# Words in the making moved to PSUM, groups of 768 columns, one more buffer, and a plan with later transposes

## The chip, the core and the metric

The kernel runs on one core of a Trainium2 chip. The metric is the time of one execution on the device, in microseconds (us): the median of the runs.

## What is computed

An attention over clusters feeds two feed-forward layers. Everything is float32 but the four weight matrices, which come as 64-bit floats.

```python
# q, k, v: (2, 8, 768, 64); centroids: (8, 16, 64)
q_assign = np.argmax(np.einsum('bhsd,hcd->bhsc', q_n, c_n), axis=-1)   # *_n: rows divided by their norm
k_assign = np.argmax(np.einsum('bhsd,hcd->bhsc', k_n, c_n), axis=-1)
mask = q_assign[:, :, :, None] == k_assign[:, :, None, :]
scores = scale * np.matmul(q, k.transpose(0, 1, 3, 2))
scores = np.where(mask, scores, -1000000000.0)
attn = np.exp(scores - np.max(scores, axis=-1, keepdims=True))
attn = attn / (np.sum(attn, axis=-1, keepdims=True) + 1e-09)
x = ...  # np.matmul(attn, v), heads joined: (1536, 512)
h = x @ w_in;   x = (h * np.cos(h)) @ w_out                  # w_in (512, 2048), w_out (2048, 512)
h = x @ w2_in;  out = (h * (1 / (1 + np.exp(-h)))) @ w2_out
```

## The kernel before

Every float32 operand is split into a high and a low float16 half, and a product is three matmuls (high by high, high by low, low by high). The 1536 tokens are 12 tiles of 128, in seven units (`UNITS`): two of one tile and five of two tiles.

All work is written as tasks with an engine, a duration, what they depend on, a priority and the buffers they take. A planner (`Graph.run`) plays them through once, in the program that builds the kernel, and the order in which it starts them is the order of the instructions on each engine, fixed. The constants in `T` are shifts of priorities and, for tasks that two engines could do, handicaps: the engine that would end first by the planner's durations, plus the handicap, gets the task. The lowest priority number goes first. `HB`, `EB`, `GB`, `WB` and `LOB` handicap VectorE (against ScalarE in the first case, GpSimd in the others), `TB` handicaps VectorE against ScalarE, `KB`, `CB` and part of `XB` handicap ScalarE, the other part of `XB` GpSimd.

Attention, per tile and head (96 in all): scores on TensorE into a PSUM buffer `pb` (L890), the maximum on VectorE (L900), two tiny steps (L904, L905), the exponential on ScalarE into a buffer `e` (L919), its high half on ScalarE or VectorE (L926, L928), its low half on GpSimd or VectorE (L933, L935), a DMA transpose of both halves issued by SP (L512) into another buffer, and the product with the values (L943, 18 matmuls into `xn_ps`). The buffers for halves and transposed halves come from one pool of eleven, `gen`, 768 columns each, of which `LEAST` keeps some for each kind. L960, L967 and L969 scale the output of a tile and split it.

Layer one, per unit (`layer1_in`, `layer1_out`): groups of `EW` = 1024 columns of the hidden layer are filled in a PSUM buffer `pb` (L1019 to L1021, 12 matmuls for each 128 rows of the hidden layer), then go through L1034 (ScalarE), L1035 (VectorE), L1037 (ScalarE, the cosine), L1040 (VectorE), L1042 (ScalarE, high half) and L1043 (GpSimd or VectorE, low half); the PSUM buffer is held until L1040. The second product goes into `g2_ps` (L1077 to L1079). Layer two (`layer2`) does the like for 512 tokens at a time, with L1200 to L1206 between its products (L1190 to L1192 and L1221 to L1223); it begins when the attention's buffers are given back, the `SWAP` task.

Weights: each of the four matrices is loaded in 16 pieces of 512 columns by 128 rows as pairs of 32-bit words, and `conv` makes a float32 of each pair: pass one on VectorE (L692) shifts the high word into the destination, pass two (L694) puts the sign and exponent bit in, and then either a third pass on VectorE adds the upper bits of the low word (L701), or ScalarE makes a number of the low word (L698) and GpSimd adds it (L699). `LOW` says for how many pieces of every four of each matrix (order: w_in, w_out, second w_out, second w_in) it is the latter. The sums that give the scale of a weight matrix are taken by TensorE (L765) or by ScalarE (L436).

PSUM: three buffers `pb` of 1024 float32 columns for scores, PE transposes, sums and the first product of both layers; `g2_ps` and `xn_ps` of 512 columns.

Of the kernel before, what the change touches and what calls it, by code (L numbers as in the profile page):

```python
# [10 lines left out]
I32 = mybir.dt.int32  # L11
# [10 lines left out]
T = dict(PW_IN=-2428, PW_OUT=-477, PW_STEP=783, W_AHEAD=-382, KV0=-981, KSTEP0=-32964, V0=33297, Q0=262, KSTEP=-17295,  # L22
         PREP=-1180, PREPQ=1313, LD=4990, LOB=-0.03, WB=-2.09, HB=1.22, EB=0.63, KB=-13.72, GB=2.92, CB=2.75, XB=1.77,
         SB=0.5, L2B=0.5, PV=-1944, HI=1053, LO=13021, XP=-1707, G1=1614, GE=-20317, GC=-1920, G2=1781, GO=-4433,
         W2=5268, XD=-9186, TB=2, WH=50.28, GATE=0)
UNITS = [(0, 0, 1), (0, 1, 1), (0, 2, 2), (0, 4, 2), (1, 0, 2), (1, 2, 2), (1, 4, 2)]

LOW = (2,2,2,2)
# [13 lines left out]
EW = 1024  # L42
NE = 4
NGEN = 11

LEAST = {'stg':2,'natk':2,'ph':4,'pT':3}
# [60 lines left out]
class Task:  # L107
    __slots__ = ("opts", "deps", "pri", "acq", "use", "lat", "table", "n", "outs", "end", "start", "tag", "port")

    def __init__(self, opts, deps, pri, acq, use, lat, table, port):  # L110
        self.opts, self.pri, self.acq, self.lat, self.table, self.port = opts, pri, acq, lat, table, port
        self.use = list(dict.fromkeys([*acq, *use]))
        self.deps = [d for d in dict.fromkeys(deps) if d is not None]
        self.outs, self.end, self.start = [], None, None


class Graph:
# [21 lines left out]
    def run(self):  # L139
# [14 lines left out]
        while done < len(self.tasks):  # L154
# [21 lines left out]
            for t in ready:  # L176
# [46 lines left out]
                done_at = t.end + t.lat + self.HOP[e]  # L223
# [46 lines left out]
def fused_kernel(tc, q, k, v, cent, w1i, w1o, w2i, w2o, out, dbg=None):  # L270
# [4 lines left out]
    P = 128  # L275
# [24 lines left out]
    with tc.manual_schedule(), tc.tile_pool(name="dram", bufs=1, space=DRAM) as dpool:  # L300
# [382 lines left out]
        def conv(dst, acc, src, shape3, pri, dst_buf=None, pool=None, deps=(), dst_deps=(), add_low=False):  # L683
# [8 lines left out]
            a = add("DVE", dve(WC, True), lambda: DV.tensor_scalar(  # L692
                d(), word(1), 3, 0x3FFFFFFF, op0=ALU.logical_shift_left, op1=ALU.bitwise_and), [l, *dst_deps], pri, acq=ex, use=[w], port=True)
            b_ = add("DVE", dve(WC), lambda: DV.scalar_tensor_tensor(  # L694
                d(), word(1), -0x40000000, d(), op0=ALU.bitwise_and, op1=ALU.bitwise_or), [a], pri - 1, use=[w, *ex], port=True)
            if add_low:

                r_ = add("ACT", act(WC, SRC), lambda: AC.activation(out=word(0), in_=word(0).bitcast(U32), func=AF.Copy, scale=2.0 ** -29), [l], pri - 2, use=[w])  # L698
                c_ = add("POOL", pool2(WC) + 0.11, lambda: PO.tensor_tensor(d(), d(), word(0), op=ALU.add), [b_, r_], pri - 2, use=[w, *ex])  # L699
            else:  # L700
                c_ = add("DVE", dve(WC), lambda: DV.scalar_tensor_tensor(  # L701
                    d(), word(0), 29, d(), op0=ALU.logical_shift_right, op1=ALU.bitwise_or), [b_], pri - 2, use=[w, *ex], port=True)
# [79 lines left out]
        def w1_prep():  # L782
# [10 lines left out]
            for i in range(NW):  # L793
                r = raw[:, i * WC:(i + 1) * WC]
                pr = PW_IN + i * 25
                c_ = conv(lambda r=r: r, None, w_in_src(w1i, i), 0, pr, None, p_wg, add_low=i % 4 < LOW[0])
# [27 lines left out]
            for d in range(ND):  # L824
# [4 lines left out]
                for c in range(4):  # L829
                    r = lambda c=c, d=d: place[d](c)  # L830
                    c_ = conv(r, None, w_out_src(w1o, d, c), WC // P, pr + c, None, p_wx if c in WXC else None, dst_deps=dd[d], add_low=c < LOW[1])
# [21 lines left out]
        def w2_convert():  # L853

            for i in range(NW):
                fb = Buf(p_w2s)
                pr = 1e6 + i * 10
                t, tq = conv(lambda fb=fb: fb.ap, w2_mx[:, i:i + 1], w2o[i * P:(i + 1) * P, :].bitcast(I32), 0, pr, fb, dst_deps=x_free if 2 in WX else (), add_low=i % 4 < LOW[2])
# [10 lines left out]
        def attention(u):  # L869
# [5 lines left out]
            for ti in range(nq):  # L875
# [4 lines left out]
                for h in range(H):  # L880
# [51 lines left out]
                    else:  # L932
# [4 lines left out]
                                   2 * NT, [tl], pr, [hb], [], [pb_], NT * b + t < PET[2])  # L937

# [162 lines left out]
        def layer2(l1_last):  # L1101
# [9 lines left out]
            for i in range(NW):  # L1111
                r = slice(i * WC, (i + 1) * WC)
                ms += conv(lambda r=r: raw(r), mx0[:, i:i + 1], w_in_src(w2i, i), 0, base + i * 10 - T["W2"], None, p_ws2, [t_swap], add_low=i % 4 < LOW[3])
# [192 lines left out]
```

## Time and profile before

| | |
|---|---|
| median of 3 runs | 826.79 us (824.79 to 829.62) |
| profiled execution, whole time | 824.2 us |
| profiled execution, first to last instruction | 822.5 us |
| TensorE busy | 715.3 us (87%), 6744 matmuls |
| VectorE busy | 541.2 us (66%), 1094 instructions |
| ScalarE busy | 490.8 us (60%), 702 |
| GpSimd busy | 230.9 us (28%), 197 |

Busy times are of the profiled execution. The share of busy time over the whole span mixes stretches with different limits: the attention with layer one up to about 560 us, and layer two alone after that. PE is TensorE's matmuls, PEld its weight loads, DVE is VectorE, ACT is ScalarE, POOL is GpSimd, SP issues the DMAs.

### The profile page before, as it was taken

What the parts mean: (1) busy time and instruction counts of PE and PEld (TensorE: products, weight loads), DVE (VectorE), ACT (ScalarE), POOL (GpSimd) and SP (SyncE); (2) the same over time, 40 slices, a digit from 0 to 9 for tenths busy, and PEclk for the clock granted to TensorE, in tenths of its full rate; (3) what the DMA queues carried; (4) which work ended last, traced back from release to release, by engine and by line L of the source; (5) the groups of instructions that cost most, each with busy time, mean ns of one, the idle gap of its engine ahead of it and who ended that gap; (6) DMA issues with size and microseconds to landing.
All of it is one profiled execution on the core that took longest, in us unless ns stands there. A gap on an engine that the chain in (4) does not pass through costs nothing.

```text
span 822.5 us, 16553 instructions
## 1 busy us (share of the span) xinstructions
PE 715.3 (87%) x6744; PEld 487.2 (59%) x6744; DVE 541.2 (66%) x1094; ACT 490.8 (60%) x702; POOL 230.9 (28%) x197
## 2 busy tenths in 40 slices
PE   2486677988779887899999999995999999999998
PEld 1353346777668765787787788882444444444443
DVE  7889988888789788989779756668670044004400
ACT  3769787888867766779659655548770045004400
POOL 3321634265452355346337323330000000000000
PEclk9967898999998999999999999997999999999999
DMA  8925799899999979978977986442312000000000
GB/s 273 358 71 160 196 196 189 148 167 187 177 183 195 248 146 174 176 194 176 183 163 127 214 183 216 141 132 75 104 51 77 26 1 0 26 26 1 0 26 26
DMA packets 233900, 111.27 MB, mean 135 GB/s; under 512 B 199520, under 2 KB 221536, under 8 KB 233824
## 3 DMA queue, kind: packets, MB, share of 16 engines
q1 hardware_dynamic: 233824, 110.23, 60.7%
q8 instruction: 52, 0.85, 0.4%
q14 instruction: 24, 0.20, 0.1%
HBM read 50.36 MB, written 10.49 MB: 74 GB/s over the span
## 4 chain that ended last, share of the span: by engine, by line
PE 58%; DVE 14%; DMA 13%; ACT 5%; issue 5%; POOL 2%; SPq 2%; POOLq 0%; DVEq 0%; ACTq 0%
DMA gen<-gen 7%; PE pb L1191 5%; PE pb L1192 5%; PE pb L1190 5%; PE pb L1019 4%; PE pb L1021 4%; PE pb L1020 4%; PE xn_ps L943 3%; PE pb L890 3%; DVE small L900 3%; PE xn_ps L1221 3%; PE g_ps L1221 3%; PE xn_ps L1223 3%; PE xn_ps L1222 3%; PE g_ps L1222 3%
## 5 line engine op out<-in xcount | busy, mean ns | idle before, releaser
L933 POOL TENSOR_TENSOR gen<-e,gen 128x768 f16<-128x768 f32 x67 | 110.0, 1656 | 63.4 <-ACT gen L926 47.3
L1078 PE MATMUL g_ps<-gT,w 128*128 128x256 f16 (+1 forms) x448 | 111.1, 260 | 3.3 <-POOL gT L1043 3.3
L919 ACT ACTIVATE e<-pb,small 128x768 f32<-128x768 f32 x96 | 94.7, 990 | 31.3 <-DVE small L905 11.9
L1019 PE MATMUL pb<-xT,w 128*128 128x256 f16 (+1 forms) x448 | 111.3, 260 | 1.8 <-DMA xT<-e 1.6
L1077 PE MATMUL g_ps<-gT,w 128*128 128x256 f16 (+1 forms) x448 | 111.2, 260 | 0.9 <-ACT x2s L1084 0.9
L1020 PE MATMUL pb<-xT,w 128*128 128x256 f16 (+1 forms) x448 | 111.2, 260 | 0.0
L1021 PE MATMUL pb<-xT,w 128*128 128x256 f16 (+1 forms) x448 | 111.2, 260 | 0.0
L1079 PE MATMUL g_ps<-gT,w 128*128 128x256 f16 (+1 forms) x448 | 111.2, 260 | 0.0
L900 DVE TENSOR_REDUCE small<-pb 128x1 f32<-128x768 f32 x96 | 89.3, 950 | 19.0 <-PE pb L890 17.0
L1202 DVE SCALAR_TENSOR_TENSOR e<-e,pb 128x1024 f32<-128x1024 f32 x24 | 29.3, 1219 | 105.2 <-ACT e L1200 105.1
L890 PE MATMUL pb<-kst,qst 96*128 96x512 f16 (+3 forms) x384 | 80.2, 343 | 18.0 <-ACT e L919 9.7
L943 PE MATMUL xn_ps<-vst,gen 128*128 128x64 f16 x1728 | 68.5, 196 | 21.5 <-DMA gen<-gen 19.8
L943 PEld LDWEIGHTS <-gen 128*128 128x128 f16 x1728 | 63.1, 100 | 33.5 <-DMA gen<-gen 26.4
L1190 PE MATMUL pb<-x2T,w 128*128 128x512 f16 x192 | 73.7, 384 | 4.5 <-ACT x2T L1170 4.5
L1043 POOL TENSOR_TENSOR gT<-e,gT 128x1024 f16<-128x1024 f32 x24 | 52.2, 2176 | 89.3 <-ACT gT L1042 80.4
L1191 PE MATMUL pb<-x2T,w 128*128 128x512 f16 x192 | 73.7, 384 | 2.5 <-DVE x2T L1172 2.5
L1192 PE MATMUL pb<-x2T,w 128*128 128x512 f16 x192 | 73.6, 383 | 0.0
L926 ACT ACTIVATE gen<-e 128x768 f16<-128x768 f32 x87 | 70.4, 840 | 2.1 <-DMA gen<-gen 0.9
L890 PEld LDWEIGHTS <-qst 128*128 128x128 f16 (+1 forms) x384 | 37.1, 101 | 41.7 <-issue 23.1
L1077 PEld LDWEIGHTS <-w 128*128 128x128 f16 x448 | 44.2, 99 | 9.8 <-issue 2.2
L1079 PEld LDWEIGHTS <-w 128*128 128x128 f16 x448 | 44.2, 99 | 7.8 <-issue 3.9
L1019 PEld LDWEIGHTS <-w 128*128 128x128 f16 x448 | 44.5, 99 | 5.6 <-DMA xT<-e 1.8
(201 smaller groups left out, 1515.0 us busy)
## 6 DMA issues: line engine op xcount, KB each, us to landing
ws<-in_moe_w_out_dram SPq DMA_DIRECT2D x24, 512.0 KB, 4.3
gT<-in_moe_w_in_dram SPq DMA_DIRECT2D x16, 512.0 KB, 5.7
ws<-in_moe_w_in_dram SPq DMA_DIRECT2D x16, 512.0 KB, 3.9
xT<-in_moe_w_out_dram SPq DMA_DIRECT2D x8, 512.0 KB, 4.8
w_dram<-x2s SPq DMA_DIRECT2D x16, 256.0 KB, 3.0
st<-w_dram SPq DMA_DIRECT2D x8, 512.0 KB, 4.4
gen<-in_k_dram SPq DMA_DIRECT2D x8, 384.0 KB, 6.7
gen<-in_v_dram SPq DMA_DIRECT2D x8, 384.0 KB, 5.2
```

What stands on the lines that cost most here:

```text
L890: PE.matmul(out=sbk.ap[:, c0:c1], lhsT=qs.ap[:kk, a, h], rhs=kb.ap[:kk, a, j].rearrange("p t c -> p (t c)")[:, c0:c1], start=(a == 1), sto ...
L900: DV.tensor_reduce(out=sm.ap[:, 0:1], in_=sbk.ap[:, :S], axis=AX.X, op=ALU.max, negate=True)
L943: PE.matmul(out=o, lhsT=hb.ap[:, pi, kt], rhs=vb.ap[:, vi, j, kt], start=(kt == 0 and pi == 0 and vi == 0), stop=(kt == NT - 1 and pi == 1 ...
L1019: PE.matmul(out=o, lhsT=wh[:, d, fs], rhs=xb.ap[:, 0, d, :n], start=(d == 0), stop=False)
L1020: PE.matmul(out=o, lhsT=wh[:, d, fs], rhs=xb.ap[:, 1, d, :n], start=False, stop=False)
L1021: PE.matmul(out=o, lhsT=wl[:, d, fs], rhs=xb.ap[:, 0, d, :n], start=False, stop=(d == ND - 1))
L1077: PE.matmul(out=o, lhsT=wh, rhs=gh, start=(f == 0 and i == 0), stop=False, skip_group_check=True)
L1078: PE.matmul(out=o, lhsT=wh, rhs=gl, start=False, stop=False, skip_group_check=True)
L1079: PE.matmul(out=o, lhsT=wl, rhs=gh, start=False, stop=(f == NF - 1), skip_group_check=True)
L1190: PE.matmul(out=o, lhsT=wh[:, d, fs], rhs=x[:, 0, d], start=(d == 0), stop=False)
L1191: PE.matmul(out=o, lhsT=wh[:, d, fs], rhs=x[:, 1, d], start=False, stop=False)
L1192: PE.matmul(out=o, lhsT=wl[:, d, fs], rhs=x[:, 0, d], start=False, stop=(d == ND - 1))
```

## The change

- `conv` gets a parameter `via`. With it, pass one writes into a PSUM buffer `pb` (512 of its columns), pass two reads and writes it there, and the last VectorE pass writes the destination. `VIA = (4,4,0,4)`, in the order of `LOW`, says for how many pieces of every four: all of w_in, w_out and the second w_in, none of the second w_out.
- `LOW` goes from (2,2,2,2) to (2,1,1,1).
- `EW` goes from 1024 to 768: the groups of layer one become three tiles of 256 columns (or six of 128), those of layer two 512 columns. The four `e` buffers get as much smaller; `gen` gets a twelfth buffer, and four instead of three are kept for transposed halves.
- In the planner a task has a field `more`: the transposes of the probabilities end 0.8 us later for what depends on them (`LATE`). It changes the plan's order alone.
- All of `T`'s constants are others.

```diff
-T = dict(PW_IN=-2428, PW_OUT=-477, PW_STEP=783, W_AHEAD=-382, KV0=-981, KSTEP0=-32964, V0=33297, Q0=262, KSTEP=-17295,
-         PREP=-1180, PREPQ=1313, LD=4990, LOB=-0.03, WB=-2.09, HB=1.22, EB=0.63, KB=-13.72, GB=2.92, CB=2.75, XB=1.77,
-         SB=0.5, L2B=0.5, PV=-1944, HI=1053, LO=13021, XP=-1707, G1=1614, GE=-20317, GC=-1920, G2=1781, GO=-4433,
-         W2=5268, XD=-9186, TB=2, WH=50.28, GATE=0)
+T = dict(PW_IN=-24521, PW_OUT=-778, PW_STEP=537, W_AHEAD=-7221, KV0=502, KSTEP0=-11826, V0=2122, Q0=-2053,
+         KSTEP=-4635, PREP=-1178, PREPQ=1321, LD=-18274, LOB=-0.79, WB=1, HB=1, EB=5, KB=-3.59, GB=1.71, CB=0.8,
+         XB=-1.49, SB=0.71, L2B=46.67, PV=-2908, HI=4830, LO=8647, XP=5755, G1=1860, GE=-4285, GC=-1560, G2=2315,
+         GO=-1529, W2=18407, XD=17052, TB=11.35, WH=-0.64, GATE=0)
+
+LATE = 0.8
...
-LOW = (2,2,2,2)
+LOW = (2,1,1,1)
+
+VIA = (4,4,0,4)
...
-EW = 1024
+EW = 768
 NE = 4
-NGEN = 11
-
-LEAST = {'stg':2,'natk':2,'ph':4,'pT':3}
+NGEN = 12
+
+LEAST = {'stg':2,'natk':2,'ph':4,'pT':4}
...
-                done_at = t.end + t.lat + self.HOP[e]
+
+                done_at = t.end + t.lat + self.HOP[e] + t.more
...
-            a = add("DVE", dve(WC, True), lambda: DV.tensor_scalar(
-                d(), word(1), 3, 0x3FFFFFFF, op0=ALU.logical_shift_left, op1=ALU.bitwise_and), [l, *dst_deps], pri, acq=ex, use=[w], port=True)
-            b_ = add("DVE", dve(WC), lambda: DV.scalar_tensor_tensor(
-                d(), word(1), -0x40000000, d(), op0=ALU.bitwise_and, op1=ALU.bitwise_or), [a], pri - 1, use=[w, *ex], port=True)
+            if via:
+
+                mb = Buf(p_pb)
+                m = lambda: mb.ap[:, :WC].bitcast(I32)
+                a = add("DVE", dve(WC), lambda: DV.tensor_scalar(
+                    m(), word(1), 3, 0x3FFFFFFF, op0=ALU.logical_shift_left, op1=ALU.bitwise_and), [l], pri, acq=[mb], use=[w])
+                to, td, tu = (d, dst_deps, ex) if add_low else (m, (), [])
+                b_ = add("DVE", dve(WC), lambda: DV.scalar_tensor_tensor(
+                    to(), word(1), -0x40000000, m(), op0=ALU.bitwise_and, op1=ALU.bitwise_or), [a, *td], pri - 1, acq=tu, use=[w, mb])
+            else:
...
             if add_low:
...
+            elif via:
+                c_ = add("DVE", dve(WC), lambda: DV.scalar_tensor_tensor(
+                    d(), word(0), 29, m(), op0=ALU.logical_shift_right, op1=ALU.bitwise_or), [b_, *dst_deps], pri - 2, acq=ex, use=[w, mb])
...
+                    if NT * b + t >= PET[2]:
+                        tt.more = LATE
```

## Rows read from the trace of the kernel before

**Rows 1.** Page of the kernel before: its span

```profile
span 822.5 us, 16553 instructions
```

**Rows 2.** Stage table of the whole span, all engines

```profile
core 0: us, PE busy (x) PEld busy (x) DVE busy (x) ACT busy (x) POOL busy (x), PEclk, DMA share, GB/s
0.00:150.00 150.00, 96.11 (x990) 64.19 (x991) 130.27 (x327) 106.99 (x156) 51.34 (x73) 0.86 0.78 206
150.00:350.00 200.00, 167.85 (x2376) 138.41 (x2374) 171.14 (x394) 151.74 (x236) 92.80 (x71) 0.96 1.01 179
350.00:500.00 150.00, 143.64 (x1721) 121.42 (x1719) 115.56 (x217) 109.67 (x168) 67.43 (x43) 1.00 0.89 183
500.00:575.00 75.00, 64.03 (x538) 52.88 (x537) 51.48 (x91) 45.22 (x70) 19.34 (x12) 0.93 0.40 127
575.00:822.50 247.50, 243.65 (x1129) 110.29 (x1127) 72.77 (x67) 77.22 (x76) 0.00 (x0) 1.00 0.09 30
```

**Rows 3.** TensorE's waits, 0 to 600 us: us in total, times, longest

```profile
PE xn_ps L943 <- DMA gen<-gen: 19.8, 20, 2.6
PE g_ps L765 <- POOL w L699: 12.2, 4, 7.7
PE pb L1190 <- ACT x2T L1170: 4.5, 1, 4.5
```

**Rows 4.** DMA transposes (line L512): us from issue to landing

```profile
DMA to landing us min/median/max: 3.1/4.4/7.0
```

**Rows 5.** Single lines of code: ns min/median/max, first and last start

```profile
L692 DVE TENSOR_SCALAR w<-ws x18: 408/424/2214, 93.2 to 556.6; 128x512 int32<-128x512 int32 x18
L694 DVE SCALAR_TENSOR_TENSOR x2s<-ws,x2s x16: 680/692/697, 141.5 to 485.3; 128x512 int32<-128x512 int32 x16
L960 DVE TENSOR_TENSOR e<-xn_ps,small x12: 679/688/692, 122.7 to 482.2; 128x512 f32<-128x512 f32 x12
L1035 DVE SCALAR_TENSOR_TENSOR e<-e,cols,pb x24: 1270/1279/1292, 149.0 to 535.9; 128x1024 f32<-128x1024 int32 x24
```

**Rows 6.** Stage table of L692, then L694 alone: VectorE busy us (instructions)

```profile
0.00:150.00 150.00, 17.76 (x33) 0.86 0.78 206
0.00:150.00 150.00, 26.49 (x33) 0.86 0.78 206
```

**Rows 7.** Timeline of GpSimd and VectorE around two moments: start us, us

```profile
41.18 1.35 POOL L699 TENSOR_TENSOR w<-w,gT 128x512 int32<-128x512 int32 x1 [3.27 <-DVE w L694]
41.42 1.66 DVE L694 SCALAR_TENSOR_TENSOR w<-gT,w 128x512 int32<-128x512 int32 x1
517.98 2.13 POOL L1043 TENSOR_TENSOR gT<-e,gT 128x1024 f16<-128x1024 f32 x1 [1.84 <-ACT gT L1042]
518.18 2.21 DVE L692 TENSOR_SCALAR w<-ws 128x512 int32<-128x512 int32 x1 [3.45 <-DMA ws<-in_moe_w_in_dram]
```

**Rows 8.** Groups by line, whole span: busy us, mean ns | idle before

```profile
L699 POOL TENSOR_TENSOR w<-w,ws 128x512 int32<-128x512 int32 x9 | 11.9, 1324 | 32.1 <-DVE w L694 30.0 <-DMA xf<-x_dram 1.5 <-issue 0.7
L698 ACT ACTIVATE ws<-ws 128x512 int32<-128x512 uint32 x20 | 13.5, 674 | 3.7 <-DMA ws<-in_moe_w_out_dram 2.1 <-DMA ws<-in_moe_w_in_dram 1.6
L1034 ACT ACTIVATE e<-pb,cols 128x1024 int32<-128x1024 f32 x24 | 26.6, 1108 | 27.8 <-PE pb L1021 25.3 <-DVE gen L935 2.4
L1040 DVE SCALAR_TENSOR_TENSOR e<-e,pb 128x1024 f32<-128x1024 f32 x24 | 29.2, 1217 | 7.7 <-ACT e L1037 7.7
L1227 ACT ACTIVATE x2s<-g_ps,cols 128x512 f32<-128x512 f32 x6 | 4.1, 687 | 48.8 <-PE g_ps L1223 48.8
L933 POOL TENSOR_TENSOR gen<-e,gen 128x768 f16<-128x768 f32 x67 | 110.0, 1656 | 63.4 <-ACT gen L926 47.3 <-DVE gen L928 8.9 <-PE pb L890 6.7
L935 DVE TENSOR_TENSOR gen<-e,gen 128x768 f16<-128x768 f32 x29 | 29.0, 1021 | 1.3 <-ACT gen L926 1.3
L969 DVE TENSOR_TENSOR e<-e 128x512 f16<-128x512 f32 x11 | 8.9, 808 | 0.0
```

**Rows 9.** TensorE's waits, 350 to 575 us alone

```profile
PE xn_ps L943 <- DMA gen<-gen: 6.3, 8, 1.2
```

## What the change should do to the time

> **What bounds the kernel now.** The span of the profiled execution is 822.5 us [rows 1]. I read the stage table first, which cuts it into five stretches [rows 2]. From 575 us to the end TensorE is busy for 243.65 of 247.5 us at full granted clock: the second layer, its queue full, VectorE and ScalarE below a third. From 350 to 500 us TensorE is busy 143.64 of 150. From 0 to 350 us it is different: VectorE is busy 130.27 of 150 and 171.14 of 200, together 301.4 of 350 (86%), TensorE less than that, and in the first 150 us its clock is granted at 0.86. So VectorE, with the chains that go through it, sets the first 350 us, TensorE everything after, with a seam at 500 to 575.
>
> The list of waits comes second [rows 3]. What TensorE loses, apart from sheer lack of work early on, is 19.8 us in 20 waits of the probability product (L943) for a transposed tile to land, 12.2 us in 4 waits of the weight sums (L765) for a GpSimd addition, and, at the seam, 4.5 us before the first matmul of layer two. There are 96 such transposes; they land 3.1 to 7.0 us after issue, median 4.4 [rows 4]: the spread is what a written-out order can't know.
>
> Third come the rows of single lines, for prices [rows 5 to 8], and the waits of the last stages alone [rows 9].
>
> **Part 1: words in PSUM (VIA).** In three of the four weight conversions, 48 of 64 pieces, the word in the making lies in a PSUM buffer between passes. Pass one (L692) has a median of 0.424 us from SBUF to SBUF [rows 5]. No row shows it into PSUM: it may stay at 0.42, or cost what a 512-column pass over PSUM costs, 0.688 us at L960 [rows 5]. I take the dear end, being the row with the same memory: +0.26 each. In the first 150 us lie 33 pieces [rows 6], 32 of them to move (all of layer one's): 32 x 0.26 = +8.4 us of VectorE.
> What comes back is lock time. At 41.18 us GpSimd begins an addition, at 41.42 a second pass (L694) that takes 1.66 instead of 0.69 us; at 517.98 another, and a first pass beside it takes 2.21 us [rows 7]. The 33 first passes before 150 us sum to 17.76 us, 3.8 above 33 x 0.424; the 33 second passes to 26.49, 3.7 above 33 x 0.69 [rows 5, 6]. L1035, one input in SBUF and one in PSUM, ran 24 times between 1270 and 1292 ns [rows 5]: never held up. So up to 7.5 us comes back, at least none; I take 7. Net +1.4 us before 150 us, bounds -7.5 to +8.4.
> The Trainium skill, "VectorE: DVE Perf Modes", section "Why PSUM operands drop a tier", speaks against this part: an fp32 operand in PSUM loses the two-fold speed. Its table of cycles for PSUM to SBUF gives, as an estimate, (120 + 512) / 0.96 = 658 ns; by that the passes cost 32 x 0.23 = +7.5 us instead of 8.4, with the same sign. No row here has shown that operation yet.
>
> **Part 2: fewer words summed on GpSimd (LOW 2,2,2,2 to 2,1,1,1).** Twelve pieces change: each loses 0.674 us on ScalarE (L698) and 1.324 us on GpSimd (L699) [rows 8] and gains a third pass of 0.69 us on VectorE. Four lie in w1_out (+2.8 us of VectorE in the first 150), four in the idle-time conversion of w2_out (+2.8 between 150 and 490), four at the seam (part 6). It shortens what the weight sums wait for: of their 12.2 us [rows 3], those before w1_in's end stay (LOW[0] is unchanged); I take 2 us of 12.2, on the path only if VectorE is not late too, so 0.
>
> **Part 3: EW 1024 to 768.** Layer one goes from 24 groups to 36: a unit of 256 tokens has six groups instead of four (the sixth of one tile), one of 128 has three instead of two. Columns stay. What is added is the fixed cost per instruction. ScalarE: 1.108 us at 1024 columns, 0.687 at 512, so 0.27 fixed [rows 8]; three of them times 12 are 9.7 us. VectorE: L1040 takes 1.217 at 1024, L960 0.688 at 512, so 0.16 fixed [rows 5, 8]; two of them times 12 are 3.8 us, half before 350. GpSimd adds little. Layer two doubles from 24 groups to 48 with 512 columns each: 48 x 0.27 + 48 x 0.16 = 20 us on engines that have 170 us to spare there [rows 2]. TensorE covers it: a group needs 12 matmuls, 2.5 us at the rate of layer two's 3 x 384 in 243.65 us. Nothing on the path; if the cover went, it would show as waits of L1190 for PSUM.
>
> **Part 4: the choices of engine (T).** The planner picks for many steps the engine that ends first plus a handicap. EB goes from 0.63 to 5: the low halves that VectorE takes (29 of 1.021 us, L935) go mostly to GpSimd, 1.656 us each (L933) [rows 8]. XB goes from 1.77 to -1.49: the 11 low halves of the attention output (0.808 us, L969 [rows 8]) leave VectorE too. HB and GB lean a little towards VectorE. I take 20 us and 9 us off, 13 back on: -16, bounds -35 to +5. GpSimd rises from 230.91 us by 20 x 1.66, less part 2's 16: it has room, being at 46% in its busiest stretch [rows 2].
> VectorE to 500 us then: +1.4 + 5.6 + 3.8 - 16 = -5 us, bounds -40 to +20. Before 350 VectorE is 86% of time, so **about -4 us** of time.
>
> **Part 5: later landing (LATE 0.8), one more general buffer (NGEN 12), four for transposed tiles.** Every planned product moves 0.8 us further behind its transpose, and SP's queue order follows. The 20 waits average 0.99 us: what 0.8 can remove lies between nothing (other waits take their place) and 16 us. In 350 to 575 us lie 6.3 us of them [rows 9] where TensorE is the bound: I take 5. Of the 13.5 before, where VectorE is late as well, I take 5. **-10 us.** A product put off holds its transposed buffer longer; the fourth one and the twelfth buffer are cover for that. Without them scores would stall behind L926.
>
> **Part 6: the seam.** The 16 conversions of layer two's first weights run beside the last unit of layer one; 16 x 0.26 + 4 x 0.69 = +7 us of VectorE, which is busy 51.48 of 75 us [rows 2], so most is covered. Fewer GpSimd steps shorten four of the chains. I take **+1 us**, bounds -6 (the 4.5 us wait and some of the slow clock, 0.93 in that stretch, gone) to +7.
>
> **Sum.** -4 - 10 + 1 = -13 us on the profiled execution's 824.2: 811.2. The median of the runs shown, 826.8, lies 2.6 above that execution, so the forecast for it is 814.
>
> **The rivals.**
> *Slower: PSUM buffers run short.* Scores, transposes, sums and layer one share three buffers of 1024 columns. Each word in the making now takes one for two or three passes, 1.4 to 2.1 us plus whatever VectorE does between. That is 48 x 2 = 96 us of one buffer, two thirds of it in the first 150 us. If TensorE then stands without a buffer in half the cases, and nothing hides it, 24 x 2 = 48; as VectorE, the bound there, would be at work on the same piece, half of that counts: +24, less the 13: about 837. It decides from the point where two other buffers are held when a word takes the third: layer one's groups hold one for fill plus four evacuations, some 8 us, so the seam is exposed too. Against it: TensorE has long gaps early that aren't for lack of PSUM. 0.24.
> *No change: waits move.* VectorE gets free, but the order is still fixed, and landing late was not the cause but the last of several things; the 19.8 us come back as waits for L919 or L926, GpSimd's 1.656 us in place of 1.021 in the chain of each tile eats the rest. 824 to 830, say 826. This is also the case in which LATE doesn't do what it says, a plan that would have the same products in the same places. 0.16.
> *More than forecast.* VectorE at -25 us with the full 16 us of landing waits: 824.2 - 22 - 16 + 2.6 = 789; half-way to my forecast, 799. 0.13.
>
> **How the numbers follow.** Forecast 0.47, with 804 to 822 as its own range. Faster by over 0.5% (below 822.7, about what a measurement of this kernel can tell): 0.47 + 0.13 = 0.60; same 0.16; slower 0.24. The range reaches half-way into the better case and half-way into the slow one and leaves out some 0.07 below and 0.12 above: 799 to 837.
>
> **What the profile after should show.** L692 and L694 writing `pb`, 0.66 to 0.69 us each, with no row above 1 us (part 1 right); at 0.42 my price was too dear. L699 at 20 instead of 32. L935 far below 29, VectorE below 300 us in the first 350. Waits of L943 for transposes under 8 us in total (part 5 right); if they are still near 20, or L890 waits as much longer, part 5 is wrong. Layer two within 1 us of 247. Wrong would be the whole if TensorE waits for conversions or PSUM buffers in the first 190 us (slow rival).

## The result and the profile after

| | before | after |
|---|---|---|
| median of 6 runs each, same chip | 827.35 us (824.79 to 829.62) | 818.98 us (818.15 to 822.83) |
| profiled execution, whole time | 824.2 us | 819.1 us |
| first to last instruction | 822.5 us | 817.4 us |

The ratio is 0.9904 (0.9878 to 0.993): about 8 us, 1.0%, faster. The forecast was 814, its range 799 to 837.

The page of after, then its stage table (columns as in [rows 2]):

```profile
span 817.4 us, 16847 instructions
...
PE 708.8 (87%) x6744; PEld 484.3 (59%) x6744; DVE 538.4 (66%) x1138; ACT 489.0 (60%) x762; POOL 298.4 (37%) x249
```

```profile
core 0: us, PE busy (x) PEld busy (x) DVE busy (x) ACT busy (x) POOL busy (x), PEclk, DMA share, GB/s
0.00:150.00 150.00, 92.97 (x903) 59.98 (x904) 127.54 (x341) 101.09 (x145) 63.59 (x89) 0.94 0.76 204
150.00:350.00 200.00, 170.91 (x2561) 145.34 (x2559) 165.57 (x381) 156.96 (x254) 116.79 (x83) 0.97 1.06 191
350.00:500.00 150.00, 145.46 (x1696) 123.14 (x1695) 109.88 (x213) 111.07 (x184) 86.42 (x58) 1.00 0.87 179
500.00:575.00 75.00, 60.95 (x488) 47.95 (x487) 59.24 (x104) 42.90 (x69) 22.43 (x14) 0.91 0.36 114
575.00:817.40 242.40, 238.55 (x1106) 107.94 (x1103) 76.13 (x101) 76.94 (x112) 9.13 (x6) 1.00 0.09 30
```

Against [rows 2]: VectorE's first 350 us fall from 301.4 to 293.1, GpSimd rises everywhere before 500 us (whole span 230.9 to 298.4), and the clock granted in the first 150 us rises from 0.86 to 0.94.

The stages are cut at fixed times and hide where the time went. Three events cut the span by work instead. They are the eighth and the twelfth (last) transpose of a tile's attention output that SP issues, and the first matmul of layer two. The rows of before, from the timelines of SP and TensorE (start us, us):

```profile
357.53 1.24 SPq L971 DMA_TRANSPOSE xT<-e  x1
...
485.46 1.24 SPq L971 DMA_TRANSPOSE xT<-e  x1
...
564.87 0.59 PE L1190 MATMUL pb<-x2T,w 128*128 128x512 f16 x1 [4.53 <-ACT x2T L1170]
```

The same in after:

```profile
349.45 1.23 SPq L992 DMA_TRANSPOSE xT<-e  x1
...
477.49 1.23 SPq L992 DMA_TRANSPOSE xT<-e  x1
...
555.88 0.59 PE L1211 MATMUL pb<-x2T,w 128*128 128x512 f16 x1 [3.74 <-ACT x2T L1191]
```

By the eighth tile after is 8.1 us ahead. The next 128.0 us are as long as before (127.9), the seam from the last transpose to layer two's first matmul goes from 79.4 to 78.4, and layer two, from that matmul to the end, from 257.6 to 261.5. So -8.0, -1.0 and +3.9 make the -5.1 of the two profiled spans.

The 8 us are not gained in the first 150 us, where most of the words are made. At the second tile's transpose after is 7.9 us behind (before first, then after), at the sixth it is level, 283.74 us against 283.32:

```profile
149.10 1.24 SPq L971 DMA_TRANSPOSE xT<-e  x1
157.04 1.48 SPq L992 DMA_TRANSPOSE xT<-e  x1
```

From the sixth to the eighth tile both kernels start the same 64 matmuls for scores and 288 into `xn_ps`, and 772 (before) and 759 (after) matmuls in all. Before needs 74.2 us for that, after 65.7 (columns as in [rows 2]), and no piece that `VIA` moves is converted there:

```profile
283.32:357.53 74.21, 62.03 (x779) 50.88 (x776) 65.26 (x154) 48.92 (x75) 31.89 (x23) 0.95 0.95 185
283.74:349.45 65.71, 60.32 (x759) 50.82 (x760) 56.58 (x142) 51.62 (x85) 37.98 (x27) 0.97 1.05 191
```

VectorE is busy 8.7 us less there. Three low halves of probabilities (L935, 2.7 us) and two of the attention output (L969, 1.4 us) have gone to GpSimd, and twelve one-column steps take a third of their time (before, then after):

```profile
L1061 DVE SCALAR_TENSOR_TENSOR cols<-cols 128x1 f32<-128x1 f32 x12 | 4.8, 471 | 0.0
L1082 DVE SCALAR_TENSOR_TENSOR cols<-cols 128x1 f32<-128x1 f32 x12 | 1.0, 154 | 0.0
```

Kernels below that share an order agree: 73.8 us in the kernel before with groups of 512 in layer two, 65.9 and 66.3 us in the two kernels on the seam. So this gain belongs to the order and the choices of engine; which of them makes it is not shown.

TensorE's waits from 0 to 600 us in after (us in total, times, longest), those that answer to [rows 3], with L1212, the second matmul group of layer two, and L908, which waits for a PSUM buffer:

```profile
PE xn_ps L964 <- DMA gen<-gen: 21.5, 21, 3.2
PE g_ps L783 <- POOL w L714: 16.0, 7, 7.9
PE pb L908 <- ACT e L937: 8.4, 7, 2.4
PE pb L1212 <- DVE x2T L1193: 6.5, 1, 6.5
...
PE pb L1211 <- ACT x2T L1191: 3.7, 1, 3.7
```

Waits for transposed tiles to land are 21.5 us, not fewer than the 19.8 of before.

The conversions in after (ns min/median/max, first and last start), to set beside [rows 5]: L701 and L704 are the first and second pass with the word in PSUM, L716 the third, L707 and L709 the first two with the word still in SBUF (the second w_out).

```profile
L701 DVE TENSOR_SCALAR pb<-ws x24: 675/689/697, 24.7 to 546.5; 128x512 int32<-128x512 int32 x24
L701 DVE TENSOR_SCALAR pb<-gT x16: 685/695/696, 5.0 to 44.8; 128x512 int32<-128x512 int32 x16
L701 DVE TENSOR_SCALAR pb<-xT x8: 675/690/714, 49.8 to 131.0; 128x512 int32<-128x512 int32 x8
L704 DVE SCALAR_TENSOR_TENSOR pb<-ws,pb x16: 678/695/697, 55.1 to 547.3; 128x512 int32<-128x512 int32 x16
L716 DVE SCALAR_TENSOR_TENSOR w<-ws,pb x13: 678/686/687, 103.3 to 548.0; 128x512 int32<-128x512 int32 x13
L707 DVE TENSOR_SCALAR x2s<-ws x16: 416/420/1616, 133.1 to 467.2; 128x512 int32<-128x512 int32 x16
L709 DVE SCALAR_TENSOR_TENSOR x2s<-ws,x2s x16: 673/684/1994, 148.4 to 467.7; 128x512 int32<-128x512 int32 x16
```

A first pass into PSUM costs 0.69 us, and none of the 48 took longer than 0.714; those that still write SBUF cost 0.42, and the longest took 1.616. And the low halves of the probabilities, against 67 and 29 in [rows 8] (busy us, mean ns): all 96 are GpSimd's.

```profile
L951 POOL TENSOR_TENSOR gen<-e,gen 128x768 f16<-128x768 f32 x96 | 159.2, 1672 | 70.4 <-ACT gen L944 27.3 <-DVE gen L946 18.5 <-issue 5.8
```

### The profile page after: what moved, and what is told of

Same layout as the page of the kernel before. It is cut to its first block, busy times and chain, and to the rows that moved or that the text cites. A ratio compares the mean times of both kernels' runs of the same rounds, so it can differ in the third digit from the quotient of the medians.

```text
span 817.4 us, 16847 instructions
## 1 busy us (share of the span) xinstructions
PE 708.8 (87%) x6744; PEld 484.3 (59%) x6744; DVE 538.4 (66%) x1138; ACT 489.0 (60%) x762; POOL 298.4 (37%) x249
## 4 chain that ended last, share of the span: by engine, by line
PE 57%; DVE 17%; DMA 13%; ACT 5%; issue 4%; POOL 2%; SPq 1%; ACTq 0%; DVEq 0%; POOLq 0%
DMA gen<-gen 8%; PE pb L1212 5%; PE pb L1213 5%; PE pb L1211 5%; PE xn_ps L964 3%; PE pb L908 3%; PE g_ps L1098 3%; PE g_ps L1099 3%; PE g_ps L1100 3%; DMA qst<-natq 3%; PE pb L1040 3%; PE pb L1042 3%; PE pb L1041 3%; PE xn_ps L1244 3%; PE xn_ps L1243 3%
## 5 line engine op out<-in xcount | busy, mean ns | idle before, releaser
L951 POOL TENSOR_TENSOR gen<-e,gen 128x768 f16<-128x768 f32 x96 | 159.2, 1672 | 70.4 <-ACT gen L944 27.3
L937 ACT ACTIVATE e<-pb,small 128x768 f32<-128x768 f32 x96 | 94.5, 988 | 25.2 <-DVE small L922 15.8
L1040 PE MATMUL pb<-xT,w 128*128 128x256 f16 (+1 forms) x448 | 108.9, 257 | 0.5 <-DVE e L1061 0.3
L1042 PE MATMUL pb<-xT,w 128*128 128x256 f16 (+1 forms) x448 | 108.9, 257 | 0.0
L1041 PE MATMUL pb<-xT,w 128*128 128x256 f16 (+1 forms) x448 | 108.9, 257 | 0.0
L1223 DVE SCALAR_TENSOR_TENSOR e<-e,pb 128x512 f32<-128x512 f32 x48 | 32.7, 684 | 94.0 <-ACT e L1221 94.0
L908 PE MATMUL pb<-kst,qst 96*128 96x512 f16 (+3 forms) x384 | 79.3, 337 | 14.7 <-ACT e L937 8.4
L964 PE MATMUL xn_ps<-vst,gen 128*128 128x64 f16 x1728 | 67.2, 196 | 21.6 <-DMA gen<-gen 21.5
L1064 POOL TENSOR_TENSOR gT<-e,gT 128x768 f16<-128x768 f32 (+2 forms) x36 | 54.5, 1523 | 67.9 <-ACT gT L1063 66.1
L1212 PE MATMUL pb<-x2T,w 128*128 128x512 f16 x192 | 73.6, 384 | 6.5 <-DVE x2T L1193 6.5
L944 ACT ACTIVATE gen<-e 128x768 f16<-128x768 f32 x81 | 66.2, 838 | 0.5 <-DMA gen<-gen 0.3
L908 PEld LDWEIGHTS <-qst 128*128 128x128 f16 (+1 forms) x384 | 36.5, 100 | 37.9 <-issue 20.7
L1227 DVE SCALAR_TENSOR_TENSOR w<-e,w 128x512 f16<-128x512 f32 x48 | 34.7, 726 | 24.6 <-ACT w L1225 24.3
L1225 ACT ACTIVATE w<-e 128x512 f16<-128x512 f32 x48 | 30.1, 628 | 31.5 <-DVE e L1223 31.4
L1098 PEld LDWEIGHTS <-w 128*128 128x128 f16 x448 | 43.9, 98 | 8.4
```

Of the source, the lines that this page charges most:

```text
L908: PE.matmul(out=sbk.ap[:, c0:c1], lhsT=qs.ap[:kk, a, h], rhs=kb.ap[:kk, a, j].rearrange("p t c -> p (t c)")[:, c0:c1], start=(a == 1), sto ...
L951: tl = add("POOL", pool2(S), lambda hi=hi, lo=lo, ex=ex: PO.tensor_tensor(lo(), ex(), hi(), op=ALU.subtract), [th], pr + T["LO"], use=[*eu ...
L964: PE.matmul(out=o, lhsT=hb.ap[:, pi, kt], rhs=vb.ap[:, vi, j, kt], start=(kt == 0 and pi == 0 and vi == 0), stop=(kt == NT - 1 and pi == 1 ...
L1040: PE.matmul(out=o, lhsT=wh[:, d, fs], rhs=xb.ap[:, 0, d, :n], start=(d == 0), stop=False)
L1041: PE.matmul(out=o, lhsT=wh[:, d, fs], rhs=xb.ap[:, 1, d, :n], start=False, stop=False)
L1042: PE.matmul(out=o, lhsT=wl[:, d, fs], rhs=xb.ap[:, 0, d, :n], start=False, stop=(d == ND - 1))
```

## The experiments

Ratios are to the kernel before on the same chip, with 95% intervals; after itself has 0.9904. In the first three kernels every other instruction keeps its place in the order of after (or of before), so that only the part named differs. In the two on the seam that holds for TensorE up to the seam, where VectorE's order changes too. In the others the planner makes a new order. Stretches are from one profiled execution each; in kernels with the same order the attention's end differs by up to 1.6 us.

### The words back in SBUF, the order kept

```diff
+        mids = [[x2s[:, :WC].bitcast(I32), x2s[:, WC:].bitcast(I32)], []]
...
-                m = lambda: mb.ap[:, :WC].bitcast(I32)
+                mid = Mid(mids[1] if isinstance(w.pool.free[0], int) else mids[0])
+                m = lambda: mid.ap()
...
+                mids[1] += [sb([P, WC], I32, f"mid2_{i}", "right") for i in range(2)]
```

> The changed kernel with its own order on every engine, but the words in the making lie in SBUF (unused columns of x2s, and two buffers made free at the seam) instead of PSUM, 48 pieces. First passes should fall from 0.69 to 0.42 us (12.5 us of VectorE less), and passes held up by GpSimd should come back (up to 11 us by the rows of before). Theory (the two cancel): within 3 us of the changed kernel's 819. Rival A (PSUM is the gain: VectorE is no longer held up): 824 or more. Rival B (PSUM only costs, the lock hardly matters in this order): 812 or less.

Measured: 835.68 us, ratio 1.0136 (1.0108 to 1.0164), 2.3% above after (1.0136 / 0.9904). The last transpose of the attention output is issued at 488.53 us, 11.0 later than in after; at the second tile it is 10.6 later already (167.67 us). Groups of this kernel (line numbers 17 higher, `x2s` and `mid` hold the words; busy us, mean ns):

```profile
L718 DVE TENSOR_SCALAR mid<-ws 128x512 int32<-128x512 int32 x16 | 11.9, 743 | 15.7 <-DMA ws<-in_moe_w_in_dram 15.6
L721 DVE SCALAR_TENSOR_TENSOR x2s<-xT,x2s 128x512 int32<-128x512 int32 x8 | 11.6, 1445 | 0.1
L721 DVE SCALAR_TENSOR_TENSOR mid<-ws,mid 128x512 int32<-128x512 int32 x12 | 10.0, 831 | 0.3
L718 DVE TENSOR_SCALAR x2s<-gT 128x512 int32<-128x512 int32 x16 | 8.7, 551 | 3.5 <-DMA gT<-in_moe_w_in_dram 3.3
...
L721 DVE SCALAR_TENSOR_TENSOR x2s<-gT,x2s 128x512 int32<-128x512 int32 x8 | 7.3, 923 | 0.1
...
L718 DVE TENSOR_SCALAR x2s<-xT 128x512 int32<-128x512 int32 x8 | 5.6, 702 | 0.0
```

The first passes are cheaper by themselves: 48 x (0.690 - 0.420) = 13.0 us. But against 0.420 us for a first pass and some 0.69 for a second, these six groups hold 16 x 0.32 + 8 x 0.75 + 12 x 0.14 + 16 x 0.13 + 8 x 0.23 + 8 x 0.28 = 19 us of standing still, and VectorE's busy time as a whole is 559.0 us against 538.4. So, in the order of after, the PSUM words are worth far more than the +1.4 us that Part 1 gave them: no other part that was priced with the order held is worth as much. But the stretch from the sixth to the eighth tile takes 65.8 us here, as in after (65.7). The words keep the first 150 us from getting slower still; the lead over the kernel before is made elsewhere.

### 29 low halves back on VectorE, the order kept

```diff
+            if t.low and e == "POOL":
+                nlow += 1
+                e = "DVE" if nlow % 10 in (1, 4, 7) else e
```

> The changed kernel with its own order, but 29 of the 96 low halves of the probabilities (three of every ten, spread evenly) are made by VectorE at the same place in the order instead of GpSimd: as many as in the kernel before. 29 x 0.95 us more on VectorE, 29 x 1.67 us less on GpSimd. Theory (VectorE's load sets the first 350 us): two thirds of 27.5 us lie there, so 8 to 16 us slower than 819. Rival (the order is what counts, neither engine's load): within 3 us, or faster, as each such chain is 0.7 us shorter.

Measured: 824.93 us, ratio 1.0016 (0.9998 to 1.0035), 1.1% or 9 us above after. VectorE is busy 132.43 and 177.46 us in the first two stages (127.54 and 165.57 in after); the last transpose is issued at 483.93 us, 6.4 later. TensorE's waits (line numbers one or two higher than in after):

```profile
PE pb L909 <- ACT e L938: 17.7, 15, 2.7
...
PE xn_ps L966 <- DMA gen<-gen: 6.0, 8, 1.6
```

This kernel waits 15.5 us less for transposes to land than after does, and is slower. That VectorE is late, so that a tile has landed before TensorE gets to it, would explain that, but was not followed tile by tile. A long list of landing waits is not a loss of its own here. From the sixth to the eighth tile it takes 67.1 us: the low halves account for 1.4 of the 8.5 us by which after is faster there than before.

### The kernel before with layer two in groups of 512

```diff
-                step = EW // N2
+                step = 1
```

> The kernel before with groups of 512 columns in layer two, 48 instead of 24, and all earlier work in the same order. Theory (TensorE covers the 20 us of added fixed cost): within 1.5 us of the kernel before, ratio 0.998 to 1.002. Rival (the finer groups start earlier at the seam, so they gain): ratio 0.994 to 0.998. Rival (VectorE's first splits at the seam compete with more small steps): ratio 1.002 to 1.006; the changed kernel's layer two is 3.9 us longer than before's.

Measured: 824.75 us, ratio 0.9996 (0.9979 to 1.0014). Twice as many groups on ScalarE and VectorE, and layer two takes 257.7 us from its first matmul (257.6 before). TensorE covers them.

### The seam: GpSimd's high halves on ScalarE

```diff
-                    alt=("POOL", pool1(c), lambda: PO.tensor_scalar(hi(), raw(), s, 1.0, op0=ALU.mult, op1=ALU.mult), T["WH"]))
+                    alt=("POOL", pool1(c), lambda: PO.tensor_scalar(hi(), raw(), s, 1.0, op0=ALU.mult, op1=ALU.mult), T["WH"] if wh is None else wh))
...
+                                     s[0], 1024, [t_sc[0]], base + i, scale_first=PRE[3][2], wh=50.28)
```

> The changed kernel with one handicap, WH, set back to 50.28 for layer two's weights alone, so ScalarE makes all their high halves; the order is the changed kernel's on TensorE and SP, and on all engines up to the seam. In the changed kernel GpSimd works at the seam (L757, L765, L766), VectorE's tiny steps beside it take 0.66 to 1.73 us instead of 0.15, and TensorE waits 3.7 + 6.5 us instead of 4.5 + 2.5 before. Theory (these GpSimd steps cost VectorE the time): 3 to 4 us faster than the changed kernel, some 815.5 us. Rival A (VectorE's order of steps is what is late, whoever is beside it): no change, 818 to 820. Rival B (ScalarE becomes the bound, seven more steps of 1.1 us): 2 to 4 us slower, 822.

What is at stake is seen in after. VectorE's scale steps, one column each, decide when `x` can be split for layer two (timeline, start us, us; GpSimd first):

```profile
551.89 2.22 POOL L757 TENSOR_SCALAR w<-w,cols 128x1024 f16<-128x1024 f32 x2 [12.78 <-DVE dmax L433]
554.08 1.12 POOL L765 TENSOR_SCALAR w<-w,cols 128x1024 f32<-128x1024 f32 x1
555.28 2.13 POOL L766 TENSOR_TENSOR w<-w 128x1024 f16<-128x1024 f32 x1
```

```profile
553.12 0.99 DVE L1186 TENSOR_TENSOR cols<-cols 128x1 f32<-128x1 f32 x1
554.15 0.15 DVE L1187 TENSOR_SCALAR cols<-cols 128x1 f32<-128x1 f32 x1
554.22 0.99 DVE L1188 SCALAR_TENSOR_TENSOR cols<-cols 128x1 f32<-128x1 f32 x1
...
555.70 1.73 DVE L410 TENSOR_TENSOR cols<-cols 128x1 f32<-128x1 f32 x1
557.35 0.15 DVE L411 TENSOR_TENSOR cols<-cols 128x1 f32<-128x1 f32 x1
```

Steps of 0.15 us take up to 1.73 and end when GpSimd's step does: 553.12 + 0.99 is 551.89 + 2.22, 555.70 + 1.73 is 555.28 + 2.13 within 0.02 us. A fourth, at 552.36, takes 0.66 us and ends between the two steps of L757. Together the four lose 0.66 + 0.99 + 0.99 + 1.73 - 4 x 0.15 = 3.8 us. From the scale being known (L450, in before L445) to the split L1193 (L1172) 9.0 us pass instead of 5.0. VectorE's other steps in between differ too, but nearly cancel: one more set of one-column steps, one weight step of 1.28 us (L768, in before L750) less. L1212 waits 6.5 us instead of before's 2.5, and layer two is 3.9 us longer.

Measured: 817.97 us, ratio 0.9928 (0.9905 to 0.9952). The wait of L1212 falls from 6.5 to 4.0 us and layer two from 261.5 to 259.2 us: the two steps of L757 are gone, those of L765 and L766 still hold VectorE (L1186 once for 2.11 us). Only about half of these 2.5 us is GpSimd's: VectorE is held 2.5 us instead of 3.8, and the rest comes from its order, in which L1193 now goes ahead of a weight step (L768) that stood before it in after. But its attention ended 1.6 us later in that execution, with the same order, and the total can't be told from after's. What follows: the hold is shown in the trace, what it costs is not shown in the time.

### The seam without GpSimd

Low halves of layer two's weights go to VectorE as well, and the scale steps of the later parts of the tokens wait for the first split of `x`.

```diff
-                t = add("DVE", 0.4, f_m, [x2done[u][0] for u in us], pr)
+                t = add("DVE", 0.4, f_m, [*[x2done[u][0] for u in us], *first_x], pr)
...
+                first_x = first_x or [tx]
```

> The changed kernel with its seam rearranged, all earlier work in the same order: layer two's weights are split without GpSimd, and the two later parts of the tokens take their scale steps only after the first part's x is split (L1193). In the changed kernel that split starts 8.4 us after the weights' scale is known, 3.5 us of it behind tiny steps of later parts and some 3 us behind GpSimd's lock. Theory (these two hold TensorE at the seam, which moving the high halves alone did not mend, as GpSimd's low halves still locked the port): 3 to 5 us faster than the changed kernel, ratio to before 0.985 to 0.988. Rival (the weights' own halves come no sooner, one wait takes another's place): ratio 0.989 to 0.993.

Measured: 824.53 us, ratio 0.9994 (0.9972 to 1.0016): 0.9% slower than after, outside what theory and rival said. TensorE's waits at layer two's start and in its second part (550 to 700 us):

```profile
PE pb L1218 <- ACT x2T L1197: 7.4, 2, 4.9
PE pb L1219 <- DVE x2T L1199: 3.8, 2, 2.0
```

L1219 waits 1.8 us at the start (4.9 for L1218) instead of 6.5, but both wait a second time, 2.5 and 2.0 us, when the second part of the tokens begins, and layer two is 264.5 us, 3.0 longer than in after. The wait was moved: within layer two these waits are 6.3 us in sum, 6.5 in after. What got longer is TensorE's own work, 253.8 us busy instead of 251.2: from 641 to 661 us, the stretch with the second pause, its clock is granted at 0.91, in after from 640 to 660 us, without a pause, at 1.00.

### Planned anew

Each of these changes one constant or group of constants; the planner then makes another order everywhere.

```diff
@@ p1
-LATE = 0.8
+LATE = 0.0
@@ p2
-LATE = 0.8
+LATE = 0.79
@@ p3
-VIA = (4,4,0,4)
+VIA = (0,0,0,0)
@@ v3
-VIA = (4,4,0,4)
+VIA = (4,4,4,4)
@@ p6
-EW = 768
-NGEN = 12
-LEAST = {'stg':2,'natk':2,'ph':4,'pT':4}
+EW = 1024
+NGEN = 11
+LEAST = {'stg':2,'natk':2,'ph':4,'pT':3}
```

Two more start from the kernel before: p8 takes over the `T` of after and nothing else, b2 `VIA = (4,4,0,4)` and nothing else.

`LATE` at nothing (p1), then almost unchanged (p2):

> The changed kernel planned with LATE 0.0 instead of 0.8, all else the same; the plan is made anew. TensorE waits 21.5 us for transposed tiles in the changed kernel against 19.8 before, so the later landing has not removed what it was to remove. Theory (LATE is not where the gain is): 816 to 823 us, waits for tiles within 5 us of 21.5. Rival (without it the waits would have grown, so it did its work): 825 or more, waits for tiles above 30 us.

> The changed kernel planned with LATE 0.79 instead of 0.8: nothing that matters in the model, but the plan is made anew and its choices can fall otherwise. It measures how much plans differ that should not. Theory (LATE 0.0 lost its 2.5 per cent at the seam, by the chance of one plan, not by tiles landing): a plan that differs in its order may well come out 3 to 15 us slower too, attention ending within 3 us of the changed kernel's 477.5 us. Rival (plans are robust, and LATE 0.8 as such was worth 2.5 per cent): within 3 us of the changed kernel, ratio 0.987 to 0.994.

No words in PSUM (p3), and all of them, the second w_out too (v3):

> The changed kernel with the words in the making in the destination as before (VIA 0,0,0,0), planned anew, so the plan knows of the lock. With the plan kept, words in SBUF cost 2.3 per cent. Theory A (PSUM words are a large part of the gain, the lock being paid in any order): ratio to before 1.00 or more, 8 us and more slower than the changed kernel. Theory B (that loss was mostly of a plan that did not know of the lock): within 4 us of the changed kernel, ratio 0.988 to 0.996.

> The changed kernel with the last matrix's words in PSUM too (VIA 4,4,4,4), planned anew: 16 conversions that run beside the attention, where passes from SBUF to SBUF were held up to 1.6, 2.0 and 2.1 us (L707, L709, L719). Theory (what PSUM words gave in the first 150 us they give here on a smaller scale, some 5 us of holding against 4 us of slower passes, and GpSimd is freer): 0 to 8 us faster than the changed kernel, ratio to before 0.980 to 0.990. Rival (between 150 and 480 us scores and layer one need the three PSUM buffers): ratio 0.993 to 1.010, with more waits of L908 for L937.

Groups and buffers as before (p6):

> The changed kernel with groups of 1024 columns, eleven buffers and three kept for transposed tiles, planned anew. Theory (the finer groups cost nothing and bring little; what shows is the spread of plans, 0.7 per cent): ratio to before 0.985 to 1.000. Rival (the twelfth buffer and the finer groups are what lets the order run): 1.005 or more.

One part of the change alone, on the kernel before (p8, b2):

> The kernel before with the new constants T alone: words in SBUF, groups of 1024, eleven buffers, two of four pieces summed on GpSimd, no later landing; planned anew. Theory (the new T loads GpSimd, and without PSUM words that holds VectorE up): ratio to before 1.005 to 1.025. Rival (the plan's constants are the gain by themselves): 0.992 or less.

> The kernel before with words in the making in PSUM (VIA 4,4,0,4) and nothing else changed, planned anew. Theory (PSUM words are worth much only where GpSimd is given more to do, as in the changed kernel: there VectorE lost 4 us before 150 us to holding, and 26 with the words in SBUF in the same order; in the kernel before it lost 12): the passes cost 8.4 us and some 8 come back, ratio to before 0.994 to 1.006. Rival (PSUM words alone are the gain): ratio 0.990 or less. Rival (they fill the PSUM buffers): 1.008 or more.

Measured, with the three stretches by work (last transpose of the attention output; from there to layer two's first matmul; layer two), each from the profiled execution:

| | time | ratio | attention to | seam | layer two |
|---|---|---|---|---|---|
| before | 827.35 | 1 | 485.5 | 79.4 | 257.6 |
| after | 818.98 | 0.9904 | 477.5 | 78.4 | 261.5 |
| p1, LATE 0 | 837.15 | 1.0150 (1.0115 to 1.0184) | 479.4 | 90.3 | 260.9 |
| p2, LATE 0.79 | 822.46 | 0.9970 (0.9945 to 0.9995) | 479.1 | 79.6 | 261.6 |
| p3, no VIA | 834.35 | 1.0112 (1.0079 to 1.0145) | 490.3 | 81.4 | 260.6 |
| v3, VIA for all | 841.93 | 1.0211 (1.0176 to 1.0247) | 487.1 | 81.9 | 268.1 |
| p6, EW 1024 | 832.16 | 1.0099 (1.0069 to 1.0130) | 480.0 | 81.4 | 269.1 |
| p8, new T on before | 843.97 | 1.0234 (1.0200 to 1.0269) | 481.5 | 97.1 | 261.1 |
| b2, VIA on before | 844.96 | 1.0247 (1.0208 to 1.0286) | 498.0 | 80.7 | 266.9 |

What follows:

- p2 changes the constant by 0.01 us and loses 0.7%. That is what another order alone can do at least, so no single figure of this table is the price of the part that it changes.
- p1 ends its attention 1.9 us after after does, little more than kernels of one order differ. Its waits for transposed tiles are 17.8 us, fewer than after's 21.5, and p2's are 14.4: the later landing took none away. What p1 loses it loses at the seam, where TensorE waits for the maximum of layer one's output, whose last weight conversions come late:

```profile
PE pb L425 <- DVE cols L1138: 9.6, 1, 9.6
```

The last third pass (L716) starts at 562.87 us there, at 548.00 in after. That is an accident of the order and not the landing that `LATE` models.

- p3 loses in the attention, 12.8 us, like the words in SBUF with the order kept (11.0), and its second passes stand still in the same way, though the planner made this order with the words in SBUF and keeps VectorE steps that it marks (`port`) apart from GpSimd's. The time is what theory A said:

```profile
L709 DVE SCALAR_TENSOR_TENSOR w<-ws,w 128x512 int32<-128x512 int32 x18 | 14.7, 820 | 0.4
L709 DVE SCALAR_TENSOR_TENSOR w<-gT,w 128x512 int32<-128x512 int32 x16 | 14.2, 890 | 0.1
L709 DVE SCALAR_TENSOR_TENSOR x2s<-ws,x2s 128x512 int32<-128x512 int32 x16 | 13.6, 850 | 0.2
```

- p6 ends its attention 2.5 us after after does. Its layer two is 7.6 us longer, and not for its wider groups, which p8 has too at 261.1 us: TensorE waits for the last part of `x` to be split, whose scale steps this order begins only at 735.6 us (timeline of TensorE):

```profile
738.79 0.38 PE L1211 MATMUL pb<-x2T,w 128*128 128x512 f16 x1 [3.19 <-ACT x2T L1191]
...
741.18 0.58 PE L1212 MATMUL pb<-x2T,w 128*128 128x512 f16 x1 [2.01 <-DVE x2T L1193]
```

In after the last split of `x` on VectorE (L1193) starts at 691.94 us, well ahead. The rest is again TensorE busy longer, 254.7 us in layer two instead of 251.2.

- v3 has the same two waits, and layer two is 6.6 us longer, the seam 3.5. But it also ends its attention 9.6 us after after does, and the loss is largest at the eighth tile (366.0 us, 349.4 in after), after a stretch in which words now lie in PSUM too. That is against the theory, and outside the rival's range as well. Scores wait for a PSUM buffer until L937 for 11.5 us (8.4 in after), which fits the rival but is too little for 9.6 us; the order is another too, and the cause stays open.
- p8 falls into the range of its theory, but not for its reason: VectorE is busy 281.4 us in the first 350, less than in before (301.4), and the attention ends 3.9 us earlier than before's. It loses at the seam, 17.7 us, most of them in one wait for the maximum of layer one's output:

```profile
PE pb L420 <- DVE cols L1117: 14.2, 1, 14.2
```

So an order from the new `T` can shorten the attention without words in PSUM; how much of after's 8 us it would give is not known.

- b2 has VectorE less busy than before in the first 350 us (294.0 against 301.4 us) and still ends its attention 12.5 us later. Waits of TensorE for a PSUM buffer that a word in the making had held are 9.7 us there (6.0 in after), too few to explain it alone. TensorE's clock is granted at 0.90 from 150 to 350 us, in before at 0.96; what that costs was not separated, and the rest stays open.

## Why the prediction was right and where it was not

The sign and the range held; the size was -8 us where -13 was forecast. The range, 799 to 837, says little: the old time lies in it. And that the size came near is partly luck: the largest term failed, and gains elsewhere stood in for it. By its steps:

**Part 1, words in PSUM.** The price of a pass was right: 0.69 us against 0.42, for 48 passes 12.9 us. The Trainium skill, "VectorE: DVE Perf Modes", section "Why PSUM operands drop a tier", is borne out by that: a first pass slows down as soon as it writes PSUM. The 658 ns estimated from that page's table, whose row is for the other direction (PSUM to SBUF), is 5% under the 0.69 measured, and the measurement decides. The lock time does not carry over: 7 us was read from [rows 5 to 7] of the order of before, where GpSimd worked 230.9 us. With 298.4 us of GpSimd work in the order of after, the six groups shown alone stand still for 19 us when the words are in SBUF, and the words' place moves the time by 2.3%. So what was forecast as a net loss of 1.4 us is, in the order of after, a part that the gain can't do without. Against the kernel before no gain of it is to be seen where most of the words are made: after is 7.9 us behind at the second tile. The Trainium skill, "SBUF — State Buffer", section "Who interferes with whom", says that a VectorE instruction with at most one input in SBUF and outside the two-port modes doesn't contend with GpSimd; the trace agrees: all three passes have one SBUF input at most, and no first pass took over 0.714 us.

**Part 2, LOW.** L714 runs 20 times (L699: 32), as expected. Its gain was put at nothing; the waits of the weight sums for it went from 12.2 to 16.0 us, in stretches where VectorE is late too. Its share wasn't separated.

**Part 3, 768 columns.** Right for layer two: the kernel before with groups of 512 there takes the same time. Layer one's groups were not measured by themselves.

**Part 4, choices of engine.** Under 300 us of VectorE in the first 350 was asked for, 293.1 came. To 500 us VectorE falls from 417.0 to 403.0 us, 14 where 5 was forecast. The low halves went entirely, not for two thirds, and putting 29 of them back costs 1.1%. So the -4 us for all terms of VectorE was too small: between the sixth and the eighth tile alone VectorE is busy 8.7 us less and the time falls by 8.5. The direction is shown by the low halves put back; how much is the choice of engine and how much the order is not. Nor is it shown that Part 4 works only together with Part 1: the two kernels with one of the parts alone are 2.5% and 2.3% slower than before, but have orders of their own, and p8, with the new `T` alone, ends its attention earlier than before.

**Part 5, later landing.** This is the step that failed. Its 10 us were the larger part of the forecast, and its test was landing waits under 8 us: they are 21.5. (The 3.1 us of [rows 4] are of another transpose on the same line; the 96 of the probabilities land after 3.7 to 7.0 us. No sum hangs on it.) Between 350 and 575 us they did fall, from 6.3 [rows 9] to 2.8 us, and the attention's length from the eighth tile on is still 128 us. Without `LATE` the waits are 17.8 us, not more, and the attention ends 1.9 us later, hardly beyond what kernels of one order differ by. And with 29 low halves on VectorE the landing waits are 6.0 us and the kernel is slower. I had taken a wait's total for what its removal gives; it was, as the "no change" rival had it, the last of several things. That rival was right on this part and wrong on the whole, because the stretch from the sixth to the eighth tile got shorter.

**Part 6, the seam.** +1 us was taken, bounds -6 to +7. The seam itself is 1.0 us shorter and layer two 3.9 longer, a net loss of 2.9 us inside the bounds; the 3.8 us for which GpSimd holds one-column VectorE steps are about the whole of the 3.9. Layer two within 1 us of its old length was therefore wrong, and for a reason that no step had priced: GpSimd now makes high halves of weights (L757, by `WH` at -0.64) and one low half (L765, L766) at just the time at which VectorE's tiny steps decide.

**The rivals.** PSUM buffers did run short, but for little: 6.0 us of waits for words before 150 us, and scores waited 8.4 us for their buffers. "More than forecast" would have needed the landing waits. (Its 799 is meant to lie half-way between 789 and 814, which is 801.5.)

**Sum by stretch.** Forecast for the attention: -14, measured -8.0. Forecast from there on: +1, measured +2.9. The first was nearer than its terms deserved, by luck: too little for VectorE (-4), too much for landing (-10).

What stays open: what `T`, layer one's `EW` with its buffers, and `LATE` are worth each, and a rival that no kernel here rules out, that most of the 8 us is the order as such and not any one part. These parts were measured only together with a new order, and each of these orders is slower than after, by 0.7% (p2) to 3.5% (b2, 1.0247 / 0.9904). None of the kernels was measurably faster than after.

## What to carry to other kernels

A price for one engine holding up another holds for one schedule: when a change gives one engine more work and takes another engine's operands out of the shared memory, judge the two together, with the load that the first will have. A sum of waits is not what their removal gives: look whether the time between two events with the same work between them got shorter, and place several such events before saying where a gain is made. Where a planner makes the order, price a part with the order held fixed, and try first what an almost unchanged constant does.

## What the runs showed of the hardware

One-column VectorE steps with two tensor inputs in SBUF stretched from 0.15 to as much as 1.73 us (2.11 in the kernel with high halves on ScalarE) beside a GpSimd step, ending with it, while the one-input step between them (L1187) stayed at 0.15. A long input isn't needed for the hold. At the seam here the held steps stand in the chain that TensorE waits for.
